# Linear attention then a gated feed-forward layer: the first three batches written in another order

## The chip, the core and the metric

The kernel runs on one core of a Trainium2 chip, as one program. The metric is device time in microseconds (us). The core has a matrix engine (TensorE, in rows PE, its weight loads PEld), VectorE (DVE), ScalarE (ACT), GpSimd (POOL, here mostly the issuer of loads) and SyncE (SP, here the issuer of stores and of transposing DMAs). Each engine runs its own instructions strictly in the order in which the program was written.

## The reference

```
phi(x) = elu(x) + 1
kv  = einsum(phi(k), v) per head;   z = sum of phi(k) over the tokens
att = (phi(q) @ kv) / (phi(q) . z + 1e-6)          # 8 batches, 8 heads, 576 tokens, 64 wide
x   = att as [4608 tokens, 512]
h   = x @ w_in                                     # 512 -> 2048
out = (h * sigmoid(beta * h)) @ w_out              # 2048 -> 512, float32
```

The inputs are float32. The kernel computes in bfloat16 with float32 sums: `h * sigmoid(beta*h)` is `silu(beta*h) / beta`, so each row of `w_out` is scaled by `1/beta` once and ScalarE's Silu does the rest.

## The kernel before, in words

**Tiling.** A batch's 576 tokens are 512 "main" tokens (four tiles of 128, t = 0 to 3) and a tail of 64 (t = 4). The eight tails are gathered in `xT_tail` and make a ninth piece of 512 tokens. For every piece there is an H phase (L282: 16 groups, ff = 0 to 15, of four 128x512 matmuls with `w_in`, each group evacuated by one Silu into `g`) and a Y phase (L307: four tiles t of 16 matmuls with `w_out`, each evacuated by one VectorE copy into `y_sb`, L319, and stored by SP, L299). Each phase is 64 matmuls. This text writes H0, Y0, H1 and so on, H8 and Y8 being the tails.

**Attention of one batch.** `elu` (L170): Exp of k and of q on ScalarE (L156), then on VectorE the max with 0 (L157), the min of the exponential with 1 (L159) and the sum (L160), for k and q each, and a copy of v beside a column of ones (L166). `attention` (L191): 20 matmuls that sum phi(k) times v (L204), masked by VectorE into `kv_bd` (L210); q transposed; for each t four "numerator" matmuls (L233) and on VectorE the denominator, its reciprocal and the product `xs` (L241, L242, L244); then `xs` transposed into `xT`, the input of H. Batches 0 and 1 transpose on TensorE (L222, L261, each evacuated by VectorE, L226, L265). From batch 2 on (`DMA_T = 2`, `by_dma`) q and `xs` are transposed by SP's DMAs (L185, L257).

**Order.** The program's order is written by hand: `h_phase` and `y_phase` call `step(fill)` after every group, and each call advances a generator of attention work by one `yield`. Batch 0's attention comes wholly before H0; batch 1's is spread from the second half of Y0 and finished by `drain` before H1; batch 2's from the start of Y1, with batch 3's `elu` beside it, both finished by `drain` before H2. For b >= 2 the attention of b+1 runs in H(b) and the `elu` of b+2 in Y(b).

**Loads and buffers.** All loads are issued by POOL, in order, with a conversion to bfloat16 (the blocks of `w_out` come as float32 into borrowed room: `g_sb[1]`, `xqk[2]` and `stage`, L106, and VectorE scales them into `w_out_sb`, L345). A POOL issue waits for the load that was issued eight before it. PSUM has four banks for H and Y (`mm`), one pair for numerators, and two for everything else. `xs` and `y_sb` have two buffers each.

## Time and profile before

| | us |
|---|---|
| median of 3 runs (lowest to highest) | 360.45 (356.15 to 363.02) |
| the profiled execution: its own time | 355.22 |
| its span in the profile | 353.4 |
| TensorE busy, of the span | 293.8 |
| VectorE, ScalarE, POOL busy | 143.7, 153.2, 48.0 |

The span runs from the first instruction to the last; the time has 1.8 us more. A busy TensorE may be running at either of its two clock levels, 1.2 or 2.4 GHz: a 128x512 matmul then takes about 0.43 or 0.22 us. The views used below are the page's parts, windows (busy time of each engine in stretches of the span), the timeline, groups of instructions by line, and waits by who waited for whom.

### The profile page before, as it was taken

To read this page: it belongs to the slowest core of one execution; us is meant where nothing else is said; L and a number is where in the kernel's file an instruction comes from. 1 tells how busy PE (TensorE), PEld (TensorE's weight loads), DVE (VectorE), ACT (ScalarE), POOL (GpSimd) and SP (SyncE) were. 2 spreads that over 40 slices of the span, in tenths; PEclk is the share of its full clock that TensorE was granted. 3 is DMA by queue.
4 is the path that set the end of the run, shared out by engine and by line. 5 is a ranking of instruction groups with operands and counts; after the bars stand their busy time and mean duration, and the time that the engine had idled before them with its cause. 6 is when DMAs were issued, how large, how long until landed. Compare 5 with 4: busy or idle time off the path is not lost.

```text
span 353.4 us, 4069 instructions
## 1 busy us (share of the span) xinstructions
PE 293.8 (83%) x1553; PEld 142.9 (40%) x1553; DVE 143.7 (41%) x281; ACT 153.2 (43%) x174; POOL 48.0 (14%) x64
## 2 busy tenths in 40 slices
...
GB/s 101 193 269 251 307 176 217 220 42 64 1 151 185 121 203 9 59 80 173 150 61 74 163 61 37 39 156 53 16 129 94 40 61 58 2 59 59 2 52 66
DMA packets 76467, 37.63 MB, mean 106 GB/s; under 512 B 44176, under 2 KB 70816, under 8 KB 76448
## 3 DMA queue, kind: packets, MB, share of 16 engines
...
q14 instruction: 7, 0.06, 0.1%
...
## 4 chain that ended last, share of the span: by engine, by line
PE 54%; DMA 9%; DVE 3%; ACT 1%; issue 1%; SPq 1%; DVEq 0%; ACTq 0%
PE h_ps L287 26%; PE y_ps L312 23%; DMA xT<-xs 4%; DMA xqk<-in_k_dram 3%; PE nps L233 2%; DMA out_dram<-y_sb 2%; PE kvp L204 2%; DVE y_sb L319 1%; SPq L185 1%; ACT e L156 1%; DVE xs L244 1%; DVE r L157 0%; DVE e L159 0%; DVE qk_p L160 0%; ACT L156 0%
## 5 line engine op out<-in xcount | busy, mean ns | idle before, releaser
L291 ACT ACTIVATE g<-h_ps,beta_c 128x512 bf16<-128x512 f32 x144 | 98.5, 687 | 107.3 <-PE h_ps L287 107.3
L287 PE MATMUL h_ps<-xT,w_in 128*128 128x512 bf16 x512 | 125.5, 396 | 7.5 <-DVE y_sb L319 4.5
L312 PE MATMUL y_ps<-w_out,g 128*128 128x512 bf16 x576 | 128.2, 382 | 0.0
L287 PEld LDWEIGHTS <-w_in 128*128 128x128 bf16 x576 | 56.1, 101 | 72.5 <-issue 16.7
L312 PEld LDWEIGHTS <-g 128*128 128x128 bf16 x576 | 56.5, 98 | 67.8 <-issue 1.7
L319 DVE COPY y_sb<-y_ps 128x512 f32<-128x512 f32 x36 | 24.5, 687 | 95.9 <-PE y_ps L312 71.6
L156 ACT ACTIVATE e<-xqk 128x2560 bf16<-128x2560 bf16 x16 | 36.7, 2331 | 4.4 <-DMA xqk<-in_q_dram 2.9
L291 ACT ACT_TABLE_LOAD x7 | 9.0, 1283 | 62.7 <-PE h_ps L287 62.7
L233 PE MATMUL nps<-kv_bd,q_pT 128*128 128x130 bf16 (+1 forms) x160 | 18.6, 247 | 18.9 <-DMA q_pT<-qk_p 10.8
L244 DVE TENSOR_TENSOR xs<-nps,rden 128x512 bf16<-128x512 f32 (+1 forms) x40 | 27.6, 690 | 7.1 <-DMA xT<-xs 5.9
L159 DVE TENSOR_SCALAR e<-e 128x2560 bf16<-128x2560 bf16 x16 | 13.3, 832 | 38.3 <-ACT e L156 38.3
L233 PEld LDWEIGHTS <-q_pT 128*128 128x128 bf16 (+1 forms) x160 | 13.2, 114 | 29.3 <-DVE xs L244 11.7
L160 DVE TENSOR_TENSOR qk_p<-r,e 128x2560 bf16<-128x2560 bf16 x16 | 23.9, 1493 | 0.5
L241 DVE TENSOR_SCALAR den<-nps 128x8 f32<-128x8 f32 (+1 forms) x40 | 6.6, 164 | 39.2 <-PE nps L233 38.8
L204 PE MATMUL kvp<-vaug,qk_p 128*128 128x130 bf16 x160 | 13.6, 243 | 8.4 <-DVE qk_p L160 8.4
L64 POOL DMA_DIRECT2D vraw<-in_v_dram x8 | 7.1, 888 | 82.7 <-DVE vaug L166 80.8
L204 PEld LDWEIGHTS <-qk_p 128*128 128x128 bf16 x160 | 12.1, 110 | 12.5 <-DVE qk_p L160 9.0
L287 PE MATMUL h_ps<-xT_tail,w_in 128*128 128x512 bf16 x64 | 14.0, 379 | 0.0
L261 PE MATMUL xtp<-identity,xs 128*128 128x128 bf16 (+1 forms) x40 | 5.4, 285 | 10.1 <-DVE xs L244 10.1
L157 DVE TENSOR_SCALAR r<-xqk 128x2560 bf16<-128x2560 bf16 x16 | 13.5, 842 | 0.0
L156 ACT ACT_TABLE_LOAD x7 | 9.0, 1283 | 8.0 <-DMA xqk<-in_k_dram 7.9
L64 POOL DMA_DIRECT2D xqk<-in_k_dram x8 | 7.5, 931 | 33.6 <-ACT e L156 20.7
...
## 6 DMA issues: line engine op xcount, KB each, us to landing
...
g<-in_moe_w_out_dram POOLq DMA_DIRECT2D x2, 1024.0 KB, 17.1
...
```

The lines of the kernel that those rows point to most:

```text
L64: nc.gpsimd.dma_start(out=dst[:, :, 0:NJ, :].rearrange("p h j d -> p h (j d)"), in_=src[b, :, 0:MAIN, :].rearrange("h (p j) d -> p h (j d) ...
L156: nc.scalar.activation(e, x, ACTF.Exp)
L157: nc.vector.tensor_scalar(r, x, 0.0, None, ALU.max)
L159: nc.vector.tensor_scalar(e, e, 1.0, None, ALU.min)
L160: nc.vector.tensor_add(st[b, "p"][:, a].rearrange("p j (h d) -> p h j d", h=H), r, e)
L204: nc.tensor.matmul(kvp[:, pp, :], qk_p[:, 1, j, p * P : (p + 1) * P], va[:, j, 2 * p : 2 * p + 2, 0 : D + 1], start=(j == 0), stop=(j == N ...
L233: nc.tensor.matmul(nps[:n, p // 2, o : o + 2 * (D + 1)], q_pT[:, t, p, :n], kv_bd[:, p, :], start=True, stop=True, skip_group_check=True,)
L244: nc.vector.tensor_mul(xs[t][:n], nv[:, :, :, 0:D], rden[:n, :, :, None].to_broadcast([n, 2, 4, D]),)
L287: nc.tensor.matmul(hp, w_in_sb[ff // 4][:, kc, (ff % 4) * P : (ff % 4 + 1) * P], x[:, :, kc, :] if b < B else x[:, kc, :], start=(kc == 0) ...
L291: nc.scalar.activation(g[:, ff, :], hp, ACTF.Silu, scale=beta_c[:, ff : ff + 1])
L312: nc.tensor.matmul(yp, g[:, ff, t * P : (t + 1) * P], w_out_sb[ff // 4][:, ff % 4, :], start=(ff == 0), stop=(ff == FC - 1),)
L319: nc.vector.tensor_copy(y_sb, yp)
```

## The change

Nothing that is computed changes. The generators and `step`, `drain`, `chain`, `wait`, `lazy` are replaced by small functions (one for each piece of a batch's attention) and by hand-written plans: dictionaries from a step of H or Y (the number of the group after which it runs) to the pieces to write there.

- Start: batch 0 is loaded as k, q, v; Exp, min and sum, and the copy of v run by halves of the heads; TensorE transposes q before and between the kv sums; the first three numerators come in a row in separate banks.
- H0 runs ff 0 to 7 for tokens t 0 and 1, then ff 0 to 7 for t 2 and 3, then ff 8 to 15 for all; the rest of batch 0's attention lies between its groups.
- `w_out` comes after batch 1's k, with batch 1's q and v between its blocks. Y0 (`y_phase_wide`) keeps four tiles open in four banks and goes by ff, so that a block of `w_out` is first needed when its ff comes up. The scaling of the four blocks is spread over H0 and Y0.
- Batch 1's attention lies in Y0, batch 2's in Y1, both with TensorE transposes (`DMA_T = 3`). From batch 3 on, q is transposed by DMA in H(b), and the numerators and the transposing DMAs of `xs` move from H(b) to Y(b).
- Transposed tiles on TensorE are evacuated by ScalarE (Copy), and so are two of Y0's four outputs.
- PSUM is four `mm` banks and four `att` banks; a tile's numerators take two `att` banks; `xs` has four buffers, `y_sb` three. VectorE's denominator and product are done by halves of the heads.

The diff, cut to its core:

```diff
-    DMA_T = 2
+    DMA_T = 3
...
-    numps = ctx.enter_context(tc.tile_pool(name="numps", bufs=1, space=bass.MemoryType.PSUM))
-    miscps = ctx.enter_context(tc.tile_pool(name="miscps", bufs=2, space=bass.MemoryType.PSUM))
+    attps = ctx.enter_context(tc.tile_pool(name="attps", bufs=4, space=bass.MemoryType.PSUM))
...
+    def mm_bank(shape, dtype=F32):
+        return mmps.tile(shape, dtype, tag="mm", name="mm")
+    def att_bank(shape, dtype=F32):
+        return attps.tile(shape, dtype, tag="att", name="att")
...
+    stage = consts.tile([P, 4 * DM], F32, name="stage")
...
+    w_out_f = [
+        a.rearrange("p (c m) -> p c m", c=4)
+        for a in (x_f[:, 0:2048], stage, g_f[:, 0:2048], g_f[:, 2048:4096])
+    ]
+    def load_w_out(i):
+        nc.gpsimd.dma_start(out=w_out_f[i], in_=w_out_v[:, i * 4 : (i + 1) * 4, :])
...
     load_k(0)
+    load_q(0)
     load_v(0)
-    load_q(0)
+    ident16 = consts.tile([FC, FC], F32)
+    make_identity(nc, ident16)
     identity = consts.tile([P, P], BF16)
     make_identity(nc, identity)
-    ident16 = consts.tile([FC, FC], F32)
-    make_identity(nc, ident16)
...
     for i in range(4):
         nc.gpsimd.dma_start(out=w_in_sb[i], in_=w_in_v[:, :, i * 512 : (i + 1) * 512])
...
-    w_out_f = [
-        a.rearrange("p (c m) -> p c m", c=4)
-        for a in (g_f[:, 0:2048], g_f[:, 2048:4096], x_f[:, 0:2048], stage)
-    ]
-    for i in range(4):
-        nc.gpsimd.dma_start(out=w_out_f[i], in_=w_out_v[:, i * 4 : (i + 1) * 4, :])
-        if i == 1:
-            load_q(1)
-            load_k(1)
+    load_k(1)
+    load_w_out(0)
+    load_w_out(1)
+    load_q(1)
+    load_w_out(2)
     load_v(1)
+    load_w_out(3)
...
+    def exp_(b, a, h0=0, h1=H):
+        if h0 == 0:
+            st[b, "e", a] = work.tile([P, H, NT, D], BF16, tag="e", name="e")
+        nc.scalar.activation(
+            st[b, "e", a][:, h0:h1], xqk[b % NX][:, a, h0:h1], ACTF.Exp
+        )
+    def relu(b, a):
+        st[b, "r", a] = work.tile([P, H, NT, D], BF16, tag="r", name="r")
+        nc.vector.tensor_scalar(st[b, "r", a], xqk[b % NX][:, a], 0.0, None, ALU.max)
...
+    def q_trans(b, t):
+        n = rows(t)
+        tp = att_bank([P, KC, P], BF16)
...
+        nc.scalar.activation(st[b, "qT"][:, t, :, :n], tp[:, :, :n], ACTF.Copy)
+    def q_trans_dma(b):
+        nc.sync.dma_start_transpose(
+            out=st[b, "qT"].rearrange("p t c n -> p (t c) n"),
+            in_=st[b, "p"][:, 0].rearrange("p j m -> p (j m)"),
+        )
...
+    def num_norm(b, t):
...
+        xs = work.tile([P, 2, 4, D], BF16, tag="xs", name="xs", bufs=4)
...
+        for i in range(2):
+            nc.vector.tensor_scalar(den[:n, i], nv[i][:, :, D], 1e-6, None, ALU.add)
+        nc.vector.reciprocal(rden[:n], den[:n])
+        for i in range(2):
...
+                xs[:n, i], nv[i][:, :, 0:D],
+                rden[:n, i, :, None].to_broadcast([n, 4, D]),
...
+        if by_dma(b):
+            nc.sync.dma_start_transpose(
+                out=x_dst(b, t), in_=xs.rearrange("p a h d -> p (a h d)")[:n]
+            )
...
+    def x_trans(b, t):
+        if by_dma(b):
+            return
...
+        nc.scalar.activation(x_dst(b, t), tp[:, :, :n], ACTF.Copy)
+    def run(plan, i):
+        for f in plan.get(i, ()):
+            f()
+    def h_phase(b, x, groups, plan):
         g = g_sb[b % 2]
...
+        for i, (ff, t0, t1) in enumerate(groups):
+            hp = mm_bank([P, 512])
+            c0, c1 = t0 * P, t1 * P
             for kc in range(KC):
                 nc.tensor.matmul(
...
+                    hp[:, c0:c1],
+                    w_in_sb[ff // 4][:, kc, (ff % 4) * P : (ff % 4 + 1) * P],
+                    x[:, t0:t1, kc, :] if b < B else x[:, kc, c0:c1],
                     start=(kc == 0), stop=(kc == KC - 1),
...
             nc.scalar.activation(
...
+                g[:, ff, c0:c1], hp[:, c0:c1], ACTF.Silu, scale=beta_c[:, ff : ff + 1]
...
+            run(plan, i)
...
+    def y_out(b, t, yp, on_act=False):
+        y_sb = work.tile([P, DM], F32, tag="y_sb", name="y_sb", bufs=3)
+        if on_act:
+            nc.scalar.activation(y_sb, yp, ACTF.Copy)
+        else:
+            nc.vector.tensor_copy(y_sb, yp)
+        store(b, t, y_sb)
+    def y_phase(b, plan):
...
+            yp = mm_bank([P, DM])
...
+                y_mm(b, yp, t, ff)
...
+                    run(plan, 4 * t + ff // 4)
+            y_out(b, t, yp)
+            run(plan, 4 * t + 3)
+    def y_phase_wide(b, plan):
+        yp = [mm_bank([P, DM]) for _ in range(4)]
+        for ff in range(FC):
+            for t in range(4):
+                y_mm(b, yp[t], t, ff)
+            run(plan, ff)
+        for t in range(4):
+            y_out(b, t, yp[t], on_act=(t % 2 == 1))
...
+    HH = H // 2
+    begin(0)
+    make_beta()
+    exp_(0, 1, 0, HH)
+    exp_(0, 1, HH, H)
+    relu(0, 1)
+    exp_(0, 0, 0, HH)
+    exp_(0, 0, HH, H)
+    phi(0, 1, 0, HH)
+    phi(0, 1, HH, H)
+    relu(0, 0)
+    phi(0, 0, 0, HH)
+    phi(0, 0, HH, H)
+    v_copy(0, 0, HH)
+    v_copy(0, HH, H)
+    q_trans(0, 0)
+    q_trans(0, 1)
+    kv_mm(0, 0, mm_bank)
+    q_trans(0, 2)
+    kv_mm(0, 1, mm_bank)
+    kv_mask(0, 0)
+    kv_mask(0, 1)
+    q_trans(0, 3)
+    q_trans(0, 4)
+    num_mm(0, 0)
+    num_norm(0, 0)
+    num_mm(0, 1)
+    num_norm(0, 1)
+    num_mm(0, 2, mm_bank)
+    num_norm(0, 2)
+    x_trans(0, 0)
+    x_trans(0, 1)
+    def F(f, *a):
+        return lambda: f(*a)
+    plan = {
+        1: [F(x_trans, 0, 2), F(num_mm, 0, 3), F(num_norm, 0, 3)],
+        3: [F(num_mm, 0, 4), F(num_norm, 0, 4)],
+        5: [F(x_trans, 0, 3)],
+        8: [F(x_trans, 0, 4)],
+        20: [F(w_out_scale, 0)],
+        22: [F(begin, 1), F(relu, 1, 1)],
+    }
+    h_phase(
+        0, xT[0],
+        [(ff, 0, 2) for ff in range(8)] + [(ff, 2, 4) for ff in range(8)]
+        + [(ff, 0, 4) for ff in range(8, FC)],
+        plan,
+    )
...
+    exp_(1, 1)
+    w_out_scale(1)
+    plan = {
+        1: [F(phi, 1, 1), F(exp_, 1, 0)],
+        5: [F(relu, 1, 0), F(w_out_scale, 2)],
+        7: [F(phi, 1, 0), F(v_copy, 1), F(load_next, 3)],
+        9: [F(q_trans, 1, 0), F(q_trans, 1, 1)],
+        10: [F(q_trans, 1, 2), F(kv_mm, 1, 0, att_bank), F(kv_mask, 1, 0)],
+        11: [F(kv_mm, 1, 1, att_bank), F(kv_mask, 1, 1), F(w_out_scale, 3),
+             F(q_trans, 1, 3), F(q_trans, 1, 4), F(num_mm, 1, 0), F(num_norm, 1, 0),
+             F(num_mm, 1, 1), F(num_norm, 1, 1)],
+        12: [F(x_trans, 1, 0), F(num_mm, 1, 2), F(num_norm, 1, 2)],
+        13: [F(x_trans, 1, 1), F(num_mm, 1, 3), F(num_norm, 1, 3)],
+        14: [F(x_trans, 1, 2), F(num_mm, 1, 4), F(num_norm, 1, 4)],
+        15: [F(x_trans, 1, 3)],
+    }
+    y_phase_wide(0, plan)
+    ALL = [(ff, 0, 4) for ff in range(FC)]
+    h_phase(1, xT[1], ALL, {
+        1: [F(x_trans, 1, 4)],
+        8: [F(begin, 2), F(relu, 2, 1)],
+        10: [F(relu, 2, 0)],
+        12: [F(v_copy, 2)],
+    })
...
+    exp_(2, 1)
+    exp_(2, 0)
+    y_phase(1, {
+        4: [F(phi, 2, 1)],
+        6: [F(phi, 2, 0)],
+        7: [F(kv_mm, 2, 0, att_bank)],
+        8: [F(kv_mask, 2, 0), F(kv_mm, 2, 1, att_bank)],
+        9: [F(kv_mask, 2, 1), F(q_trans, 2, 0), F(q_trans, 2, 1)],
+        10: [F(q_trans, 2, 2), F(q_trans, 2, 3)],
+        11: [F(q_trans, 2, 4), F(begin, 3), F(exp_, 3, 1), F(exp_, 3, 0), F(num_mm, 2, 0), F(num_norm, 2, 0)],
+        12: [F(num_mm, 2, 1), F(num_norm, 2, 1)],
+        13: [F(num_mm, 2, 2), F(num_norm, 2, 2), F(x_trans, 2, 0)],
+        14: [F(num_mm, 2, 3), F(num_norm, 2, 3), F(x_trans, 2, 1)],
+        15: [F(x_trans, 2, 2), F(x_trans, 2, 3)],
+    })
...
+        n = b + 1
+        plan = {}
+        if b == 2:
+            plan[0] = [F(num_mm, 2, 4), F(num_norm, 2, 4)]
+            plan[2] = [F(x_trans, 2, 4)]
+        if n < B:
+            plan[3] = [F(relu, n, 1), F(phi, n, 1)]
+            plan[5] = [F(relu, n, 0), F(phi, n, 0), F(q_trans_dma, n)]
+            plan[7] = [F(v_copy, n)]
+            plan[11] = [F(kv_mm, n, 0, att_bank)]
+            plan[12] = [F(kv_mask, n, 0), F(kv_mm, n, 1, att_bank)]
+            plan[13] = [F(kv_mask, n, 1)]
+        h_phase(b, xT[b % 3] if b < B else xT_tail, ALL, plan)
...
+        plan = {}
+        if n + 1 < B:
+            begin(n + 1)
+            exp_(n + 1, 1)
+            exp_(n + 1, 0)
+        if n < B:
+            for t in range(NT):
+                plan[1 + 2 * t] = [F(num_mm, n, t)]
+                plan[2 + 2 * t] = [F(num_norm, n, t)]
+        y_phase(b, plan)
```

**What moves on POOL, the issuer of loads,** from the last two blocks of `w_in` on. In the names, `xqk_73` and `vraw_76` before (`xqk_70` and `vraw_73` after) are batch 1's q, k and v. Before:

```order
L100 DMA w_in_81<-in_moe_w_in_dram 128x4x512
L100 DMA w_in_82<-in_moe_w_in_dram 128x4x512
L111 DMA g_92<-in_moe_w_out_dram 128x4x512 x2
L64 DMA xqk_73<-in_q_dram 128x8x256
L68 DMA xqk_73<-in_q_dram 64x8x64
L64 DMA xqk_73<-in_k_dram 128x8x256
L68 DMA xqk_73<-in_k_dram 64x8x64
L111 DMA xqk_74<-in_moe_w_out_dram 128x4x512
L111 DMA stage<-in_moe_w_out_dram 128x4x512
L64 DMA vraw_76<-in_v_dram 128x8x256
```

and after the change:

```order
L118 DMA w_in_78<-in_moe_w_in_dram 128x4x512
L118 DMA w_in_79<-in_moe_w_in_dram 128x4x512
L70 DMA xqk_70<-in_k_dram 128x8x256
L74 DMA xqk_70<-in_k_dram 64x8x64
L103 DMA xqk_71<-in_moe_w_out_dram 128x4x512
L103 DMA stage<-in_moe_w_out_dram 128x4x512
L70 DMA xqk_70<-in_q_dram 128x8x256
L74 DMA xqk_70<-in_q_dram 64x8x64
L103 DMA g_89<-in_moe_w_out_dram 128x4x512
L70 DMA vraw_73<-in_v_dram 128x8x256
L74 DMA vraw_73<-in_v_dram 64x8x64
L103 DMA g_89<-in_moe_w_out_dram 128x4x512
```

Batch 1's k is now ahead of `w_out`, and its q and v stand between the blocks.

**What moves on VectorE around Y0:** `L345` before and `L160` after are the scaling of `w_out`, `e`, `qk_p` and `r` are the elu of batch 1. Before:

```order
L345 TENSOR_SCALAR w_out_83<-g_92,rbeta 128x512 x4
L345 TENSOR_SCALAR w_out_84<-g_92,rbeta 128x512 x4
L345 TENSOR_SCALAR w_out_85<-xqk_74,rbeta 128x512 x4
L345 TENSOR_SCALAR w_out_86<-stage,rbeta 128x512 x4
L84 MEMSET xqk_74 64x16x32
L319 COPY y_sb<-y_ps 128x512
L157 TENSOR_SCALAR r<-xqk_73 128x2560
L319 COPY y_sb<-y_ps 128x512
L166 COPY vaug_78<-vraw_76 128x8x5x64
L159 TENSOR_SCALAR e<-e 128x2560
L160 TENSOR_TENSOR qk_p<-r,e 128x8x5x64
L157 TENSOR_SCALAR r<-xqk_73 128x2560
```

and after the change:

```order
L160 TENSOR_SCALAR w_out_80<-xqk_71,rbeta 128x512 x4
L185 TENSOR_SCALAR r<-xqk_70 128x2560
L90 MEMSET xqk_71 64x16x32
L160 TENSOR_SCALAR w_out_81<-stage,rbeta 128x512 x4
L189 TENSOR_SCALAR e<-e 128x2560
L190 TENSOR_TENSOR qk_p<-r,e 128x8x5x64
L185 TENSOR_SCALAR r<-xqk_70 128x2560
L160 TENSOR_SCALAR w_out_82<-g_89,rbeta 128x512 x4
L189 TENSOR_SCALAR e<-e 128x2560
L190 TENSOR_TENSOR qk_p<-r,e 128x8x5x64
L196 COPY vaug_75<-vraw_73 128x8x5x64
L216 TENSOR_TENSOR kv_bd<-att,kvmask 128x260 x2
L160 TENSOR_SCALAR w_out_83<-g_89,rbeta 128x512 x4
L264 TENSOR_SCALAR den<-att 128x4 x2
```

The third block's scaling (`w_out_82`) now stands behind batch 1's `qk_p` for k, which needs its Exp, and the fourth's behind the masks of the kv sums.

**What moves on SP around Y1 and H2:** before, from Y0's and Y1's first stores on:

```order
L299 DMA out_dram<-y_sb 128x512 x5
L185 DMA_TRANSPOSE q_pT<-qk_p 128x20x128
L299 DMA out_dram<-y_sb 128x512 x2
L257 DMA_TRANSPOSE xT_89<-xs 128x4x128 x2
L185 DMA_TRANSPOSE q_pT<-qk_p 128x20x128
L299 DMA out_dram<-y_sb 128x512
L257 DMA_TRANSPOSE xT_89<-xs 128x4x128 x2
L257 DMA_TRANSPOSE xT_tail<-xs 128x4x64
```

and after the change:

```order
L319 DMA out_dram<-y_sb 128x512 x8
L236 DMA_TRANSPOSE q_pT<-qk_p 128x20x128
L272 DMA_TRANSPOSE xT_84<-xs 128x4x128
L319 DMA out_dram<-y_sb 128x512
L272 DMA_TRANSPOSE xT_84<-xs 128x4x128 x2
L319 DMA out_dram<-y_sb 128x512
L272 DMA_TRANSPOSE xT_84<-xs 128x4x128
L272 DMA_TRANSPOSE xT_tail<-xs 128x4x64
```

All eight stores of Y0 and Y1 now come ahead of the first transposing DMA, which is batch 3's.

## Rows read from the trace of the kernel before

**Rows 1.** The page: its first line and part 1's TensorE row.
```profile
span 353.4 us, 4069 instructions
...
PE 293.8 (83%) x1553; PEld 142.9 (40%) x1553; DVE 143.7 (41%) x281; ACT 153.2 (43%) x174; POOL 48.0 (14%) x64
```

**Rows 2.** Windows by stage: busy us (instructions) per engine, TensorE clock, DMA share, GB/s.
```profile
0.00:32.00 32.00, 10.07 (x82) 7.85 (x82) 20.14 (x49) 7.24 (x4) 17.20 (x28) 1.00 1.18 204
32.00:47.70 15.70, 15.70 (x67) 6.76 (x66) 7.50 (x18) 10.31 (x15) 5.94 (x7) 1.00 1.35 251
47.70:61.40 13.70, 13.70 (x65) 6.21 (x64) 7.98 (x10) 7.82 (x5) 6.95 (x9) 1.00 1.50 206
61.40:75.20 13.80, 7.73 (x83) 5.70 (x80) 10.86 (x28) 0.00 (x0) 0.72 (x2) 0.68 1.23 171
75.20:91.50 16.30, 16.30 (x67) 6.94 (x66) 1.76 (x3) 10.31 (x15) 1.57 (x2) 0.85 0.32 37
91.50:132.70 41.20, 19.36 (x106) 9.10 (x105) 20.10 (x33) 11.21 (x6) 8.93 (x10) 0.78 1.04 142
132.70:263.30 130.60, 125.60 (x673) 60.74 (x674) 60.37 (x111) 72.09 (x80) 6.67 (x8) 0.97 0.45 82
263.30:293.40 30.10, 30.10 (x169) 14.78 (x168) 8.72 (x21) 12.18 (x17) 0.00 (x0) 1.00 0.28 79
293.40:349.40 56.00, 55.28 (x257) 24.85 (x254) 6.22 (x9) 22.00 (x32) 0.00 (x0) 1.00 0.13 38
```

**Rows 3.** Timeline, first 43 us: start, length, instruction, [idle before, and releaser].
```profile
7.94 1.28 ACT L156 ACT_TABLE_LOAD   x1 [7.94 <-DMA xqk<-in_k_dram]
...
11.34 1.13 DVE L166 COPY vaug<-vraw 128x2560 bf16<-128x2560 bf16 x1 [2.23 <-DMA vraw<-in_v_dram]
...
14.44 2.34 ACT L156 ACTIVATE e<-xqk 128x2560 bf16<-128x2560 bf16 x1 [2.87 <-DMA xqk<-in_q_dram]
...
27.49 0.89 POOL L64 DMA_DIRECT2D vraw<-in_v_dram  x1 [1.91 <-DMA g<-in_moe_w_out_dram]
...
30.18 0.69 POOL L68 DMA_DIRECT2D vraw<-in_v_dram  x1 [1.80 <-DMA g<-in_moe_w_out_dram]
...
39.79 1.67 DVE L345 TENSOR_SCALAR w_out<-xqk,rbeta 128x512 bf16<-128x512 f32 x4 [4.23 <-DMA xqk<-in_moe_w_out_dram]
...
42.25 1.89 DVE L345 TENSOR_SCALAR w_out<-stage,rbeta 128x512 bf16<-128x512 f32 x4 [0.79 <-DMA stage<-in_moe_w_out_dram]
```

**Rows 4.** The page, part 5: costliest groups, with mean ns of one.
```profile
L291 ACT ACTIVATE g<-h_ps,beta_c 128x512 bf16<-128x512 f32 x144 | 98.5, 687 | 107.3 <-PE h_ps L287 107.3
...
L156 ACT ACTIVATE e<-xqk 128x2560 bf16<-128x2560 bf16 x16 | 36.7, 2331 | 4.4 <-DMA xqk<-in_q_dram 2.9
...
L159 DVE TENSOR_SCALAR e<-e 128x2560 bf16<-128x2560 bf16 x16 | 13.3, 832 | 38.3 <-ACT e L156 38.3
...
L160 DVE TENSOR_TENSOR qk_p<-r,e 128x2560 bf16<-128x2560 bf16 x16 | 23.9, 1493 | 0.5
...
L241 DVE TENSOR_SCALAR den<-nps 128x8 f32<-128x8 f32 (+1 forms) x40 | 6.6, 164 | 39.2 <-PE nps L233 38.8
```

**Rows 5.** Groups by line with shapes kept apart, the same columns.
```profile
L244 DVE TENSOR_TENSOR xs<-nps,rden 128x512 bf16<-128x512 f32 x32 | 22.1, 692 | 5.6 <-DMA xT<-xs 4.6
...
L265 DVE COPY xT<-xtp 128x512 bf16<-128x512 bf16 x8 | 3.4, 425 | 3.7 <-PE xtp L261 3.7
...
L345 DVE TENSOR_SCALAR w_out<-g,rbeta 128x512 bf16<-128x512 f32 x8 | 3.2, 479 | 0.0
```

**Rows 6.** Waits, all engines: us in total, times, longest.
```profile
PE nps L233 <- DMA q_pT<-qk_p: 10.8, 1, 10.8
...
DVE y_sb L319 <- DMA out_dram<-y_sb: 19.7, 4, 6.7
...
PE h_ps L287 <- DVE y_sb L319: 4.5, 2, 3.0
```

**Rows 7.** The tile q_pT: time from issue to landing of its transposes.
```profile
DMA to landing us min/median/max: 4.9/6.1/11.9
```

258 lines of the change are left out of this document (82 added, 176 removed).

## The prediction

> **What bounds the kernel now.** First the page's head: TensorE is busy 293.8 of 353.4 us [rows 1]. The last four phases, with no attention beside them, take 55.28 us for 257 matmuls, 13.8 a phase, 0.86 a group of four [rows 2]; eighteen such phases are 249 us. So the bound is TensorE at full clock, and some 100 us lie beside it. Next the windows by stage, to see where [rows 2]: 32.0 us pass before H0, in which TensorE is busy for 10; H0 and the main part of Y0 run without a gap; 13.8 us of batch 1's attention stand alone (7.7 busy, granted clock 0.68); then comes H1; then Y1 with batch 2's attention takes 41.2 where its matmuls need 13.8. From H2 on there is little left: 130.6 us for eight phases with four batches of attention, and a clean pair H6, Y6 with one batch's attention inside is 30.1. Last the waits: in Y1 a numerator stood 10.8 us for q's transposing DMA, output copies stood 19.7 us in four waits for their store to free a buffer, and H phases stood 4.5 us behind such copies [rows 6]. The reader should see three lumps: the start, the attention between Y0 and H1, and Y1.
>
> **Start, up to H0.** q0 takes v0's place in the load queue, so k0 is there at 7.9, q0 at 11.3, v0 at 14.4 [rows 3]. ScalarE: table load 1.28, then four half Exps of 2.33/2 [rows 3, 4]: 9.2, 10.4, 11.6, 12.7, 13.9. VectorE: a half of min and sum is (0.83 + 1.49)/2 = 1.16 [rows 4]; k's halves end at 11.6 and 12.8, the max of q (0.83, taken as the min's) at 13.6, q's halves at 14.8 and 16.0, v's copy (1.13 [rows 3]) at 17.1. TensorE then does 20 transposes and 20 sums at the lower clock, 0.12 each (H6's pair has 40 such matmuls in 30.1 - 27.6 = 2.5 us, 0.06 each, at the upper one [rows 2]): 16.1 + 4.8 = 20.9, the first numerators 21.4. A tile's norm is now two denominators, a reciprocal and two half products: 0.16 x 2 + 0.2 + 0.69 [rows 4, 5] and 0.2 for starting two more instructions, 1.45. Two norms end at 24.3, the second transpose and its copy at 25.6. H0 starts at **25.6**, not 32.0.
>
> **ScalarE's copies.** No row shows a Copy on ScalarE. The nearest are VectorE's copy of the same tile, 0.43 [rows 5], and ScalarE's own Silu of the same width, 0.69 [rows 4]; I take 0.69, the same engine. On the path lie one before H0, one before H1 and four before H2, so the lower end would take 6 x 0.26 = 1.6 us off. The Trainium skill, "ScalarE: Activation LUTs", Rules for kernel authors, says to leave such plain operations to VectorE, as faster per element; by its figure for immediate scale (186 ns + 0.833 ns per element, section What ACT_TABLE_LOAD costs) a copy is an estimated 0.61 us, and the sum would be 0.5 us lower. That VectorE is faster speaks against this part, yet VectorE is what Y0 will wait for, and 0.43 x 12 copies there would cost more than they do on ScalarE.
>
> **H0.** 13.8, plus the 1.9 that the low clock cost H0 before (15.7 - 13.8 [rows 2]), plus twelve transposes and eight numerators between the groups at 0.12: 18.1, to 43.7. The half-width groups stream the same columns. In sum H0 ends 4 us earlier, not 6.4, as 2.4 of attention went inside.
>
> **Y0 and batch 1's attention.** Weight blocks land every 2.7 us and a q, k or v every 3.5 [rows 3]. From the end of w_in (24.8) the new order lands k1 28.3, w_out blocks 31.0 and 33.7, q1 37.1, block 2 39.8, v1 43.3, block 3 46.0: no load is late. But block 2 is scaled behind batch 1's phi(k) in VectorE's queue, and that Exp is behind all of H0's Silus. ScalarE: last Silu 44.6, table 45.9, Exps 48.2 and 50.5. VectorE: phi(k) 50.6, max 51.4, block 2 (4 x 0.48 [rows 5]) 53.3, phi(q) 55.6, v 56.5. TensorE: eight ff's end at 50.9; ff 8 waits for its slice, 51.9; after ff 9 (53.7) q's transposes wait for phi(q), 55.7; transposes, sums, ff 10 and 11 take it to 59.4. VectorE: masks 60.2, block 3 62.0, norms of two tiles 64.9, then three rounds of numerators, norm and handing over (0.25 + 1.45 + 0.2), 70.6, and the first output copy 0.69. H1 could begin at 71.9; in that stretch TensorE is idle by turns, as it was at 61.4 to 75.2, where the clock was at its lower level for part [rows 2]. Hidden in part by VectorE's chain, I add 1.6 (bounds 0 and 5): **73.5**, against 75.2.
>
> **H1 and Y1.** H1: 13.8, 0.2 for a transpose, and 1.7 for a slow start (bounds 0 and the 2.5 of before, 16.3 - 13.8 [rows 2]): 89.2. Y1 needs no DMA any more, so the 10.8 us wait goes. Eight groups and half the sums: 96.7; three groups, the other sums, 16 transposes: 100.9; one group, four transposes, the first numerators: 102.2. Now VectorE has an output copy (0.69) and four norms (5.8): 108.7. ScalarE meanwhile has batch 3's two Exps (102.8 to 107.5) ahead of four transposed tiles' copies, 2.8, so the last is there at 110.4. H2 starts at **110.6**, against 132.7: this stage gives 20 of the total.
>
> **H2 to the end.** Five pairs at 30.1 [rows 2] and 0.6 for batch 2's last tile: 151.1, against 160.7 from 132.7 to 293.4. The 9.6 are the waits for output buffers [rows 6], which go as q's long transposing DMA leaves the store's place on SP and `y_sb` has a third buffer, and H2's slow start. In Y each norm (1.45) has two groups (1.7) to hide behind. Then four phases, 56.0, and the tail, 4.0, as before.
>
> **Sum.** 25.6 + 18.1 + 29.8 + 15.7 + 21.4 + 151.1 + 56.0 + 4.0 = 321.7 of span, 1.8 around it: 323.5, against the profiled execution's 355.22. The median shown, 360.45, is 5 higher than that; part of that spread may come from the DMA waits that go, so I say **324**, and the range has room for the shift.
>
> **Rivals.**
> A, *q's transposes land late*. From batch 3 on q's DMA is issued some 7.1 us into H (a copy, then 2 x (0.83 + 2.32)) and needed 13.8 + 1.2 + 1.7 = 16.7 in: 9.6 us of slack. At the same place VectorE's copy of v frees the loads of three batches (v, k, q) on POOL. For it: landing took 4.9 to 11.9, the most beside loads [rows 7]; against it: the median is 6.1, and only three of the five have loads beside them. 3 x 2.3 = 7: **331**. The Trainium skill, "Trainium Kernel Development and Optimization", Key Constraints, says that DMAs from SP's and POOL's queues share the same 16 engines and interleave; by it A is to be expected, and the spread from 4.9 to 11.9 agrees.
> B, *the clock stays low* in Y0's second half and Y1's. For it: 0.68 and 0.78 in the two stages of interleaved attention [rows 2]. Against it: Y1's first half is dense, and the 0.78 held an 11 us wait that goes. Eight ff's at twice 0.86 are 6.9 more in Y0, as many in Y1, half behind VectorE: **331**.
> C, *Y0 runs as its blocks land*, as if VectorE's order did not hold them: H1 at 62.5, **312**. Against it: the order shows block 2 behind phi(k).
> D, *slower*: the late transposes of A as long as the one in Y1 before, 10.8 of waiting [rows 6], for each of five batches: 54 us, **377**. It outweighs the gain from a mean wait of 7.4 us a batch, thus from a landing of 17 us. Against it: no landing was over 11.9 [rows 7].
>
> **Numbers.** Forecast 0.64, A 0.15, B 0.11, C 0.05, D 0.05, of which 0.03 come out slower and 0.02 within 2%, about what a measurement here can tell from no change. The forecast's own bounds: the low clock's costs at nothing (-3.3), copies at 0.43 (-1.6) and no slow start at H0 (-1.9) give 317; nothing gained from H2 on (+9.6) 333, the median's shift another 3. Range 313 to 336, which takes in A and B. Faster 0.95, same 0.02, slower 0.03.
>
> **What would show it.** H0 from about 25.6; in Y0 a TensorE wait after ff 9 for phi(q); H1 near 73, H2 near 110 with ScalarE's copies behind batch 3's Exps; pairs of 30.1 from there. Wrong if numerators wait for `q_pT` in each Y (A), if Y0's matmuls take 0.43 us (B), or if H2 begins after 120.

## The result, and the profile after

The changed kernel takes **319.16 us** (median of 4 runs, 319.0 to 322.8) against 358.55 (median of 4, 356.15 to 363.02) in the same comparison: a ratio of 0.8946, 95% interval 0.8838 to 0.9053. Ratios leave out runs that are over 1.5% above the fastest of their kernel (here the one of 363.02), medians do not. The forecast was 324, range 313 to 336. The profiled execution's span is 317.0 us against 353.4 [rows 1]. First the head of the page after and part 1's TensorE row:

```profile
span 317.0 us, 4289 instructions
...
PE 286.5 (90%) x1625; PEld 144.0 (45%) x1625; DVE 142.9 (45%) x344; ACT 168.5 (53%) x216; POOL 46.7 (15%) x64
```

TensorE has 72 matmuls more (40 transposes of batch 2, 32 halves in H0) and is busy 7.3 us less, as it was granted the upper clock for more of its time (mean granted clock 0.987 for 0.942); the rest of the 36.4 us was idle time. Next the windows of the kernel after by stage, with the columns of [rows 2]; the stages are the start, H0, Y0 in two parts, H1, Y1, the pair H2 and Y2, four pairs, and the last phases:

```profile
0.00:24.60 24.60, 7.45 (x62) 5.87 (x63) 15.47 (x45) 9.85 (x13) 14.45 (x25) 1.00 1.19 163
24.60:41.60 17.00, 17.00 (x116) 11.27 (x116) 7.31 (x21) 14.18 (x27) 6.60 (x8) 0.90 1.31 294
41.60:53.60 12.00, 9.16 (x42) 3.82 (x41) 7.33 (x10) 6.59 (x5) 4.62 (x5) 1.00 1.48 227
53.60:68.50 14.90, 12.47 (x101) 7.52 (x102) 10.10 (x34) 5.03 (x10) 4.97 (x6) 0.89 1.58 190
68.50:84.05 15.55, 14.42 (x68) 6.30 (x69) 2.69 (x4) 12.15 (x19) 1.56 (x2) 1.00 0.58 109
84.05:103.90 19.85, 18.78 (x138) 10.18 (x137) 12.39 (x30) 15.61 (x16) 3.48 (x4) 1.00 0.63 101
103.90:136.40 32.50, 31.25 (x177) 15.05 (x177) 16.69 (x42) 18.16 (x21) 4.70 (x6) 1.00 0.80 125
136.40:257.10 120.70, 120.70 (x674) 59.16 (x672) 64.69 (x152) 64.93 (x77) 6.27 (x8) 1.00 0.50 97
257.10:312.40 55.30, 55.24 (x256) 24.85 (x254) 5.55 (x9) 22.00 (x32) 0.00 (x0) 1.00 0.13 39
```

Against [rows 2]: the start is 7.4 us shorter (24.6 for 32.0). From H0 to Y1's first matmul nothing is gained: 59.45 for 59.5. Y1 is 21.35 shorter (19.85 for 41.2), the five pairs from H2 on 7.5 (153.2 for 160.7), the end as long as before. 7.4 + 0 + 21.4 + 7.5 = 36.3 of the 36.4.

Now the two places that the forecast named. Y0 in the timeline of the kernel after (start, length, instruction, idle time before it and what ended that):

```profile
42.53 1.28 ACT L179 ACT_TABLE_LOAD   x1
43.83 4.57 ACT L179 ACTIVATE e<-xqk 128x2560 bf16<-128x2560 bf16 x2
46.20 0.83 DVE L189 TENSOR_SCALAR e<-e 128x2560 bf16<-128x2560 bf16 x1 [10.34 <-ACT e L179]
...
49.20 2.06 DVE L160 TENSOR_SCALAR w_out<-g,rbeta 128x512 bf16<-128x512 f32 x4
...
50.05 1.89 PE L328 MATMUL mm<-w_out,g 128*128 128x512 bf16 x8 [1.06 <-DVE w_out L160]
...
53.59 0.62 PE L228 MATMUL att<-identity,qk_p 128*128 128x128 bf16 x8 [1.65 <-DVE qk_p L190]
```

ScalarE is through with H0's Silus at 42.5, so VectorE stands 10.34 us for the Exp of k before it can do phi(k), and block 2 of w_out is scaled behind that. TensorE waits 1.06 for its slice, goes on to ff 9, and waits 1.65 for phi(q): the wait that the prediction put there, after ff 9. And the place before H2:

```profile
97.24 4.55 ACT L179 ACTIVATE e<-xqk 128x2560 bf16<-128x2560 bf16 x2
101.69 2.14 ACT L292 ACTIVATE xT<-att 128x512 bf16<-128x512 bf16 x4
...
103.89 1.02 PE L305 MATMUL mm<-xT,w_in 128*128 128x512 bf16 x4 [0.95 <-ACT xT L292]
```

Four transposed tiles' copies follow two Exps of batch 3 without a gap, and H2's first matmul waits for the last of them, as forecast. One wait was not forecast, in H1. Y0's four outputs come at once and `y_sb` has three buffers:

```profile
68.31 0.59 ACT L336 ACTIVATE y_sb<-mm 128x512 f32<-128x512 f32 x1
71.05 0.60 ACT L336 ACTIVATE y_sb<-mm 128x512 f32<-128x512 f32 x1 [2.14 <-DMA out_dram<-y_sb]
71.66 1.28 ACT L311 ACT_TABLE_LOAD   x1
...
71.69 1.02 PE L305 MATMUL mm<-xT,w_in 128*128 128x512 bf16 x4 [0.15 <-ACT y_sb L336]
73.69 1.67 PE L305 MATMUL mm<-xT,w_in 128*128 128x512 bf16 x7 [0.98 <-ACT g L311]
```

ScalarE's second output copy stands 2.14 us for a store, ahead of H1's table load and Silus in the same queue; TensorE then finds no free bank and waits 0.15 and 0.98 us.

Last the waits in the kernel after (us in total, times, longest), which answer to [rows 6]:

```profile
PE att L228 <- DVE qk_p L190: 11.0, 3, 8.4
...
ACT y_sb L336 <- DMA out_dram<-y_sb: 2.1, 1, 2.1
...
PE att L248 <- DMA q_pT<-qk_p: 1.2, 1, 1.2
```

And of the kernel after, as in [rows 7], the view of the tile `q_pT`, time from issue to landing:

```profile
DMA to landing us min/median/max: 4.9/8.7/10.2
```

The wait of 10.8 us, for batch 2's q, is gone with its DMA; the one that is left is 1.2, for batch 3's, in Y2. The first row is the wait for phi(q), 8.4 of its 11.0 us at the start and 1.65 in Y0. The output copies' 19.7 us and TensorE's 4.5 us behind them are gone but for the place in H1. The landing itself is no faster: the median went from 6.1 us (six transposes) to 8.7 (five).

### The profile page after: what moved, and what is told of

It reads as the page before. It is cut to its first block, busy times and chain, and to the rows that moved or that the text cites. A ratio compares the mean times of both kernels' runs of the same rounds, so it can differ in the third digit from the quotient of the medians.

```text
span 317.0 us, 4289 instructions
## 1 busy us (share of the span) xinstructions
PE 286.5 (90%) x1625; PEld 144.0 (45%) x1625; DVE 142.9 (45%) x344; ACT 168.5 (53%) x216; POOL 46.7 (15%) x64
## 4 chain that ended last, share of the span: by engine, by line
PE 80%; DVE 6%; DMA 6%; ACT 5%; issue 2%; POOL 0%; ACTq 0%; DVEq 0%; POOLq 0%
PE mm L305 37%; PE mm L328 35%; DMA q_pT<-qk_p 3%; PE att L248 3%; ACT e L179 3%; PE att L208 2%; DMA xqk<-in_k_dram 2%; DVE qk_p L190 1%; PE att L228 1%; DVE w_out L160 1%; DVE e L189 1%; ACT xT L292 1%; PE att L288 1%; ACT L179 1%; DMA out_dram<-y_sb 1%
## 5 line engine op out<-in xcount | busy, mean ns | idle before, releaser
L328 PE MATMUL mm<-w_out,g 128*128 128x512 bf16 x576 | 133.5, 381 | 1.2 <-DVE w_out L160 1.1
L311 ACT ACTIVATE g<-mm,beta_c 128x512 bf16<-128x512 f32 (+1 forms) x152 | 98.0, 666 | 54.2 <-PE mm L305 53.9
L305 PE MATMUL mm<-xT,w_in 128*128 128x512 bf16 (+1 forms) x544 | 116.2, 369 | 3.4 <-ACT xT L292 2.3
L338 DVE COPY y_sb<-mm 128x512 f32<-128x512 f32 x34 | 23.4, 690 | 91.1 <-PE mm L328 91.0
L179 ACT ACTIVATE e<-xqk 128x2560 bf16<-128x2560 bf16 (+1 forms) x18 | 36.7, 2091 | 0.1
L267 DVE TENSOR_TENSOR xs<-att,rden 128x256 bf16<-128x256 f32 (+1 forms) x78 | 29.4, 418 | 1.3
L190 DVE TENSOR_TENSOR qk_p<-r,e 128x2560 bf16<-128x2560 bf16 (+1 forms) x18 | 24.2, 1345 | 0.6
L189 DVE TENSOR_SCALAR e<-e 128x2560 bf16<-128x2560 bf16 (+1 forms) x18 | 13.5, 751 | 11.9 <-ACT e L179 11.9
L248 PE MATMUL att<-kv_bd,q_pT 128*128 128x130 bf16 (+1 forms) x156 | 17.0, 234 | 1.9 <-DMA q_pT<-qk_p 1.2
L305 PE MATMUL mm<-xT_tail,w_in 128*128 128x512 bf16 x64 | 14.0, 379 | 0.0
## 6 DMA issues: line engine op xcount, KB each, us to landing
xqk<-in_q_dram POOLq DMA_DIRECT2D x8, 512.0 KB, 11.6
```

The costliest lines, as they stand in the source:

```text
L179: nc.scalar.activation(st[b, "e", a][:, h0:h1], xqk[b % NX][:, a, h0:h1], ACTF.Exp)
L189: nc.vector.tensor_scalar(e, e, 1.0, None, ALU.min)
L190: nc.vector.tensor_add(st[b, "p"][:, a].rearrange("p j (h d) -> p h j d", h=H)[:, h0:h1], st[b, "r", a][:, h0:h1], e,)
L248: nc.tensor.matmul(nps[:n, pp * 2 * (D + 1) : (pp + 1) * 2 * (D + 1)], st[b, "qT"][:, t, p, :n], st[b, "kv"][:, p, :], start=True, stop=Tr ...
L267: nc.vector.tensor_mul(xs[:n, i], nv[i][:, :, 0:D], rden[:n, i, :, None].to_broadcast([n, 4, D]),)
L305: nc.tensor.matmul(hp[:, c0:c1], w_in_sb[ff // 4][:, kc, (ff % 4) * P : (ff % 4 + 1) * P], x[:, t0:t1, kc, :] if b < B else x[:, kc, c0:c1 ...
```

## Experiments: from the kernel before

Experiments 1, 2, 4 and 5 ran on one chip, 6 to 9 on a second, 3 and 10 to 12 on a third, each time beside the kernel before. The changed kernel did not run beside them, so against it stand the ratios and the spans of the profiled executions.

**1. One number, DMA_T.** Batch 2's q and x transposed on TensorE, all else as before.

```diff
-    DMA_T = 2
+    DMA_T = 3
```

> The kernel before with one number changed: batch 2 is transposed on TensorE too, with the old generators, two-bank pool and two buffers. Theory W (waits): most of Y1's 41.2 us was time spent waiting for transposing DMAs, 10.8 us for q and about 8 for xs and xT, so the stage from Y1 to H2 falls to 24 to 30 us and the whole is 11 to 17 us faster (ratio 0.955 to 0.97). Rival O (order): the gain of the whole change comes from the hand-written plans; the old drain still leaves batch 2's attention alone after Y1, as batch 1's 13.8 us were, so the stage stays above 35 us and the whole is within 2% of before.

339.67 us (337.53 to 341.17), ratio 0.9447 [0.9365, 0.9529] to the kernel before: theory W, and rival O falls. The window from Y1 to H2:

```profile
91.20:120.90 29.70, 20.27 (x143) 10.86 (x145) 23.19 (x42) 11.28 (x7) 8.60 (x10) 0.94 1.06 135
```

It takes 29.7 us in place of 41.2, though its 40 matmuls of transposes and their copies come on top. The span fell by 14.4 us (to 339.0), within the 11 to 17 expected; the ratio is lower than the 0.955 to 0.97.

**2. One number, the buffers of `y_sb`.**

```diff
-            y_sb = work.tile([P, DM], F32, tag="y_sb", name="y_sb")
+            y_sb = work.tile([P, DM], F32, tag="y_sb", name="y_sb", bufs=3)
```

> The kernel before with three output buffers instead of two. Theory W: the 19.7 us of output copies waiting for a store go, and with them the 4.5 us that H phases waited; five pairs from H2 on fall from 160.7 to 154 or less, the whole is 4 to 8 us faster. Rival S (the queue of SP): stores stand behind q's transposing DMA, which holds SP for 3 to 6 us, so a third buffer only moves the wait to the next copy; less than 2 us of gain.

352.77 us, ratio 0.9831 [0.9772, 0.989]. Windows of Y1 and of the five pairs, then TensorE's wait and the row of the tile `q_pT`:

```profile
91.90:136.50 44.60, 19.26 (x103) 9.10 (x103) 20.09 (x33) 11.25 (x7) 8.92 (x10) 0.75 1.03 131
136.50:290.60 154.10, 153.13 (x830) 74.96 (x841) 69.69 (x132) 84.22 (x97) 6.65 (x8) 0.98 0.44 85
...
PE nps L233 <- DMA q_pT<-qk_p: 14.1, 1, 14.1
...
DMA to landing us min/median/max: 4.9/6.1/15.2
```

The five pairs take 154.1 us for 160.7: W, and rival S falls. Y1, which had to stay as it was, became 3.4 us longer (44.6): the transposing DMA that it waits for landed after 15.2 us, where it took 11.9 before [rows 7], and TensorE stood 14.1 us for it, for 10.8. Why it landed later was not tried.

**3. Both numbers.**

> The kernel before with two of its numbers changed: DMA_T 3 (batch 2's transposes on TensorE) and three buffers of y_sb; nothing else of the change. Alone, the first took the span from 353.4 to 339.0 and the second the five pairs from H2 to Y6 from 160.7 to 154.3. Theory W (both take away waits of their own place): they add. Y1's start to H2 stays near 30, the five pairs fall from 158.0 to 152.5-154.5, span 333-336, time 333-337, so some 23-26 of the 39 us of the change come from two numbers. Rival D (what one takes away, the other's wait comes back in its place, since both are set by SP's queue): time 338-341, five pairs still 157-158.

336.44 us (336.16 to 337.96), ratio 0.9472 [0.9416, 0.9529]. Windows of this kernel: start, H0 to Y1, Y1 to H2, five pairs.

```profile
0.00:32.40 32.40, 10.08 (x82) 7.87 (x82) 20.18 (x49) 7.24 (x4) 17.80 (x28) 1.00 1.19 205
32.40:91.50 59.10, 53.06 (x273) 25.69 (x273) 28.20 (x58) 28.40 (x35) 14.79 (x18) 0.88 1.07 163
91.50:121.10 29.60, 20.18 (x142) 10.87 (x143) 23.19 (x42) 11.24 (x7) 8.59 (x10) 0.94 1.04 133
121.10:274.50 153.40, 152.30 (x833) 74.45 (x841) 69.99 (x133) 84.22 (x97) 6.70 (x8) 0.99 0.47 90
```

The pairs are down to 153.4, as in the changed kernel, and Y1 to H2 to 29.6: theory W, and rival D falls. By the spans of the profiled executions the two numbers are worth 18.8 us (353.4 to 334.6) of the whole change's 36.4, by the ratios 5.3% of 10.5%: half of it, less than the 23 to 26 of 39 us expected. What is left between this kernel and the changed one is 17.6 us of span: 7.8 before H0 and 9.8 in Y1 to H2. Experiments 6 and 7 take the first further apart. The second was not taken apart: the order of the work, ScalarE's copies and the PSUM banks all differ there, and which of them brings it is open.

## Experiments: from the changed kernel

**4. Two buffers of `y_sb`, as before** (`bufs=3` to `bufs=2`).

> The changed kernel with two output buffers instead of three. Theory S' (SP's order is what counts): with q's DMA moved into H nothing long stands before a store, so two buffers cost only at the end of Y0, where four outputs come at once: H1 is held 2 to 4 us longer, pairs from H3 on stay at 30.2. Theory W: the third buffer is what took the waits of the pairs away; pairs go back to 31 to 33, the whole is 7 to 10 us slower.

320.29 us, ratio 0.8923 [0.887, 0.8977], which can't be told from the changed kernel's. The pairs stay at 30.2 us from H3 on: theory S'. H1 takes 16.4 us for 15.6, held 0.8 longer and not the 2 to 4 expected. So here the third buffer isn't what frees the H phases: with SP's new order two suffice, as q's long DMA no longer stands between the copies and their stores (that it is this move, and not another of the order's, is argued and was not tried by itself). In experiment 2 the third buffer sufficed with the DMA in its old place. Each cures the same wait, and together they gain no more than one.

**5. Every evacuation on VectorE** (both `nc.scalar.activation(..., ACTF.Copy)` of transposed tiles become `nc.vector.tensor_copy`, and Y0's outputs too).

> The changed kernel with all evacuations of transposed tiles, and two outputs of Y0, back on VectorE. Theory V (VectorE bounds Y0): copies of 0.43 us come into the chain of norms; the stretch from q's transposes in Y0 to H1 (14.9 us) grows by 2 to 4, Y1's by 0 to 2, the whole is 2 to 5 us slower. Rival (plain copies belong on VectorE, where one takes 0.43 and not 0.60): the handing over gets shorter, Batch 3's Exps no longer stand ahead of the copies, and the whole is 0 to 3 us faster.

318.74 us, ratio 0.8888 [0.8829, 0.8948], 0.6% under the ratio of the changed kernel with intervals that overlap: no difference that can be told. Theory V, that it would cost 2 to 5 us, is not borne out; its trace does not rule out a smaller cost. In it H0 starts 0.5 us later (TensorE waits 1.53 in place of 0.69 for VectorE's copy of x) and H2 1.6 earlier; the pair H2 to Y2 then waits 2.6 us for `q_pT`, in place of 1.2, and takes 33.7 for 32.4 (from H2's first matmul to H3's). H0's 15.3 us, for 17.0, is no gain of the copies: it had the granted clock at 1.00 throughout, while the changed kernel's was 0.50 (1.2 GHz) from about 25.3 to 28.7, after waits of 0.55 and 0.69 us that experiment 11 had as well, without a drop; experiment 12, with the same copies as here, has 17.0 again. The clock was 1.00 in Y0 too, worth another 1.6 us (see 6). So of some 3.3 us that the clock gave, H2's start shows 1.6.

**6. H0 in full width**: the numerators of all five tiles of batch 0 and four of their five transposes ahead of sixteen groups of 512 columns, no halves.

```diff
...
-        [(ff, 0, 2) for ff in range(8)] + [(ff, 2, 4) for ff in range(8)]
-        + [(ff, 0, 4) for ff in range(8, FC)],
+        [(ff, 0, 4) for ff in range(FC)],
```

> The changed kernel with H0 in full width: all four token tiles are transposed before its first group. Theory H (halves pay little): H0 starts 2 to 4 us later but has 1.5 to 2.5 us less of attention inside, so Y0 starts 0.5 to 2 us later and the whole is 0 to 2 us slower. Rival: the halves bring the whole 7.4 us by which H0 starts earlier; the whole is 4 us or more slower.

318.71 us (median of three runs, 317.92 to 319.57; a fourth took 777.22, and no trace tells why), ratio 0.8919 [0.8874, 0.8964]: theory H, and the rival falls. H0 starts 2.2 us later, Y0 0.7, and H1 comes 1.2 us *earlier*. The windows from the end of phi(q) to H1, first of the changed kernel, then of this one:

```profile
53.53:68.47 14.94, 12.45 (x101) 7.51 (x101) 10.14 (x34) 5.00 (x10) 4.97 (x6) 0.89 1.58 190
...
53.91:67.23 13.32, 10.85 (x100) 6.71 (x101) 10.08 (x34) 4.99 (x10) 4.97 (x6) 1.00 1.58 192
```

The same instructions take 14.9 us at a mean granted clock of 0.89 (it was 0.50 from 62.8 to 66.3) and 13.3 at 1.00. With these 1.6 us taken out H1 would come 0.4 later here, so the halves bring H0 forward and hardly anything behind it. Whether they caused that clock was not tried; 4 and 7, which have them, show 0.89 and 0.88 in this place, 5, 9 and 10, which have them too, 1.00.

**7. The old order of loads** (k, v, q; blocks 0 and 1 of w_out, then q1 and k1, blocks 2 and 3, v1).

> The changed kernel with the load order of before: k, v, q for batch 0, and batch 1 behind the first two blocks of w_out, v last. Theory L (only the first three loads count): q of batch 0 lands 3.1 us later, H0 starts 1.5 to 3 us later; around Y0 no load was late, so the stretches from H0 to H2 stay within 0.7 us; the whole is 1 to 3 us slower. Rival: batch 1's place among the w_out blocks is needed for Y0's attention; Y0 to H1 grows by 3 us or more.

320.91 us, ratio 0.8978 [0.8945, 0.9011]. H0 2.2 us later and all behind it shifted by 1.6 to 2.4 (span 319.4 for 317.0): theory L, by the trace; the ratio alone does not tell it from the changed kernel. Experiments 6 and 7 took back 2.2 us each of the start's 7.4; the other 3 were not taken apart.

**8. Y0 tile by tile**, with all of w_out scaled ahead of batch 1's elu (`y_phase` in place of `y_phase_wide`, `w_out_scale(2)` and `(3)` before the plan).

> The changed kernel with Y0 one tile after the other, as in other batches, and all scaling of w_out ahead of batch 1's elu on VectorE. Theory E (what ends Y0 is phi(q), then the chain of norms, not the landing of w_out): TensorE waits about 2 us for block 3 in the first tile, phi(q) is ready at the same time as now (53 to 54), and two of VectorE's scalings are out of the chain of norms; H1 starts within 1.5 us of 68.5, the whole within 1%. Rival (the wide Y0 earns its four banks): Y0 stands until block 3 is scaled, and H1 starts 4 us or more later.

316.02 us, ratio 0.8837 [0.879, 0.8885]: theory E, and better. H1 came 2.6 us earlier and H2 4.0, of which the next pair gave 2.4 back (34.8 us). Phi(q) was ready 0.75 later (54.3); from there to H1 it took 11.6 us for 14.9. Of these 3.3 us 1.6 goes with the granted clock, 1.00 here (see 6), and most of the rest with block 3's scaling, 2.07 us that no longer stand ahead of the norms. H1 itself took 14.1 for 15.6, as Y0's outputs no longer come at once. The timeline of the next pair:

```profile
108.61 3.26 SPq L236 DMA_TRANSPOSE q_pT<-qk_p  x1
...
119.51 0.41 PE L248 MATMUL att<-kv_bd,q_pT 128*128 128x130 bf16 x4 [1.98 <-DMA q_pT<-qk_p]
119.75 3.09 PE L328 MATMUL mm<-w_out,g 128*128 128x512 bf16 x8
```

q's DMA is issued once phi(q) is done, and TensorE waits 1.98 us for it, then runs the next eight matmuls in 3.09 us, which take 1.89 at the upper clock.

**9. Block 2 scaled ahead of phi(k)**, Y0 still over four banks.

```diff
+    w_out_scale(2)
...
-        5: [F(relu, 1, 0), F(w_out_scale, 2)],
+        5: [F(relu, 1, 0)],
```

> The changed kernel with block 2 of w_out scaled ahead of batch 1's phi(k) on VectorE, where VectorE is idle for 10.3 us. Theory Q (VectorE's queue is what holds Y0): the wait of 1.1 us for w_out goes, phi(q) is ready 2 us earlier, H1 starts 1.5 to 2.5 us earlier and the whole is as much faster. Rival (ScalarE holds it: Exp of q ends at 48.4, and the chain of norms sets the end): H1 starts less than 0.7 us earlier.

319.5 us, ratio 0.8938 [0.8888, 0.8988]: theory Q's first half, and not its second. H1 started at 65.1 for 68.5, more than the 1.5 to 2.5 us expected: phi(q) was ready 1.35 earlier (52.2), and 1.6 of the rest goes with the clock, 1.00 in Y0 here (see 6). And H1 lost it: 19.6 us for 15.6.

```profile
70.42 0.60 ACT L336 ACTIVATE y_sb<-mm 128x512 f32<-128x512 f32 x1 [4.88 <-DMA out_dram<-y_sb]
...
71.07 1.02 PE L305 MATMUL mm<-xT,w_in 128*128 128x512 bf16 x4 [2.88 <-ACT y_sb L336]
```

The four outputs come 3.4 us earlier, but the store whose buffer the last one needs landed 5.3 us after issue, where it took 2.5: 4.88 us of standing where it was 2.14.

**10. The same with four buffers of `y_sb`.**

> The changed kernel with w_out's block 2 scaled ahead of phi(k) of batch 1, as before, and four buffers of y_sb in place of three. With three, H1 was reached 3.4 us earlier, but took 19.7 us in place of 15.6, with ScalarE's output copy 4.88 us behind a store. Theory B (the buffer was the wait): each of Y0's four outputs has its own, H1 is back to 15.6-16.0, Y1 starts at 80.5-81.5, H2 at 100-101.5; the span falls to 313.5-315.5, as the next place (q_pT's landing in Y2) gives back some 2. Rival H (the stores would hold ScalarE or TensorE in another way): H1 stays at 18-20, span 317-318.

313.64 us (312.93 to 314.15), ratio 0.8819 [0.877, 0.8868]. Theory B, and better: the span is 312.4 for the 313.5 to 315.5 expected. The rows of the same place:

```profile
64.66 1.08 ACT L336 ACTIVATE y_sb<-mm 128x512 f32<-128x512 f32 x2
65.76 1.28 ACT L311 ACT_TABLE_LOAD   x1
```

Both copies follow each other without a wait; H1 takes 14.1 us (15.6 to 16.0 expected), Y1 starts at 79.0, and the pair H2 to Y2 takes 32.9, with 1.8 us for `q_pT`.

**11. Experiment 8, and q ahead of k from H2 on.**

```diff
-            plan[3] = [F(relu, n, 1), F(phi, n, 1)]
-            plan[5] = [F(relu, n, 0), F(phi, n, 0), F(q_trans_dma, n)]
+            plan[3] = [F(relu, n, 0), F(phi, n, 0), F(q_trans_dma, n)]
+            plan[5] = [F(relu, n, 1), F(phi, n, 1)]
```

> The changed kernel with Y0 tile by tile and w_out scaled first, as in the run before, and from H2 on q's elu and its transposing DMA ahead of k's. There the DMA of q_pT was issued at 108.6, when phi(q) was done, and TensorE waited 1.98 us for it at 117.5, then ran 3 us at the lower clock; the pair H2 to Y2 took 34.8 us, where 30.2 is the pair without waits. Theory G (gains of the early stages are given back at q_pT's landing): issued 2.5-3 us earlier, it lands before it is wanted; the pair takes 30.2-32.0, the span is 311.5-313.5, time 312-314. Rival C (the DMA engines are busy with the loads of batch 5 there, and it lands when those are through): the wait stays over 1 us, the pair 33.5-35, time 315.5-317; phi(k) being later could also make TensorE wait at H's step 11 for it (rival K: a new wait of 0.5-1 us in each of five H phases, time 316-320).

313.4 us (312.78 to 314.71), ratio 0.8816 [0.8764, 0.8868]. Theory G: the pair takes 30.9 us for 34.8, without a wait for `q_pT` or, in any H, for phi(k) (so no K). The DMA's issue at 107.02 stands 5.7 us into H2, where it stood 8.7 in experiment 8. The pair's window, and a row from the tile's view:

```profile
101.30:132.20 30.90, 30.79 (x174) 15.03 (x176) 16.69 (x42) 18.16 (x21) 4.70 (x6) 1.00 0.85 132
...
DMA to landing us min/median/max: 4.9/5.7/6.5
```

Issued 3.9 us ahead of the loads that v's copy frees, it lands in 4.9 to 5.9 us for the three batches that have such loads, where it took 8.8 to 10.8 in experiment 8. In this trace Y0 began 2.2 us earlier than in 8 (H0 at 1.00) and waited it out, 3.71 us for block 3, which is scaled when it has landed, at 45.64 in both. Behind that wait the granted clock was 0.50 from 46.9 to 50.3, and phi(q) and H1 came 1.4 us later than in 8: what this run gains on 8 it gains in the pair. A narrow Y0 can't begin its first tile's end before that; the wide one can.

**12. Experiment 11 with VectorE's evacuations and four buffers.**

> As the run before (Y0 tile by tile, w_out scaled first, q's elu and DMA ahead of k's), with every evacuation of a transposed tile on VectorE and four buffers of y_sb. VectorE's evacuations alone had brought H0's length down by 1.7, Y0's by 1.0 and H2's start by 1.6, and all was given back in the pair H2 to Y2. Theory G (it was given back at q_pT's landing, and nowhere else): with that wait gone these are kept, H2 at 97-99, span 308.5-311.5, time 309-312. Rival V (VectorE is the longer queue in Y0 once w_out's 16 scalings stand ahead): TensorE waits more for phi(q) and for xs in Y0 and Y1, H2 at 99.5-101, time 312-315, no better than the run before it.

315.15 us (314.22 to 316.55), ratio 0.8874 [0.8813, 0.8935], 1.75 us over 11 in the same comparison: theory G falls, and rival V fits, by the time and by H2, which starts at 100.8, for 101.3, not at 97 to 99. The row of TensorE's waits that grew:

```profile
PE mm L305 <- DVE xT L292: 4.1, 3, 1.5
```

With the copies on VectorE, x's last tiles stand behind four norms and an output copy, and H0, H1 and H2 each wait for them (2.3 us in 11, for ScalarE's). The two profiled executions are 314.22 and 314.71, so the traces show how it comes about and not the 1.75.

The two fastest, 10 and 11, beat both kernels: spans of 312.4 and 312.9 us for the changed kernel's 317.0, though the intervals of their ratios still touch its own. Their gains lie in different places (Y0, where 1.6 is the clock's, and H1; Y2), and q ahead of k on top of 10 was not run; from 32.9 and 30.9 for the pair, an estimate is 2 us less than 313.6.

## Why the prediction was right, and where its sizes were off

**Start.** H0 at 24.57 for 25.6. The norm of a tile was taken as 1.45 (its terms make 1.41, and no row shows the 0.2 for starting two more instructions); the second one shows 0.22 + 0.20 + 0.76 = 1.18, and 1.26 from start to end. Transposes ran earlier than the sum had them (q's from 15.2, for 16.1). The order of the loads was worth 2.2 of the 7.4 (7).

**ScalarE's copies.** A Copy of 128x512 from PSUM took 0.60 us, the nearest row taken was Silu's 0.69, and VectorE's is 0.43. The Trainium skill, "ScalarE: Activation LUTs", What ACT_TABLE_LOAD costs, gave an estimate of 0.61: the trace agrees. The Trainium skill's rule on the same page, Rules for kernel authors, to use VectorE for relu, max, min, add and mul, which the prediction took to hold for a copy too, was not borne out here: experiment 5 was no faster that could be told, and 12 was slower. That the engine with the shorter queue at that place decides, and not the price, fits 12's waits and was not shown apart.

**H0, Y0 and batch 1.** H0 17.06 for 18.1. The 1.9 in it for a low clock was there: 17.06 is 1.7 above the 15.35 of experiment 5. [rows 2] has a clock of 1.00 in H0 of the kernel before, but its matmuls show the slow start that the prediction took from its length (ns of one: shortest, median, longest):

```profile
L287 PE MATMUL h_ps<-xT,w_in x9: 577/634/634, 32.0 to 35.4; 128*128 128x512 bf16 x9
...
L287 PE MATMUL h_ps<-xT,w_in x18: 379/379/379, 36.2 to 39.9; 128*128 128x512 bf16 x18
```

The first nine start 0.43 us apart, the next 18 0.22, which are the two clock levels; so a 1.00 in that column alone does not show the upper one.

Y0 to H1 took 26.84 for 29.8. The order of waits was right to the instruction, and phi(q) was ready 11.9 us after Y0's start, as forecast; it came at 53.5 and not 55.6 because Y0 began earlier. What was too long lay behind it, 14.9 us for 17.9. The three rounds of numerators and norm were taken as 5.7 with 1.6 for a low clock on top; they took 5.7 with a low clock in them, and 4.1 without it in experiment 6. So the 1.6 was of the right size, and the rounds were not. Two norms took 2.4 for 2.9, and 0.6 lies between the 71.9 written and the 71.3 that 70.6 and 0.69 make. Y0 did stand behind VectorE, thus rival C (312) fell; experiment 10, with block 2 ahead of phi(k) and a buffer for each output, comes near its time, and 1.6 of that goes with the clock.

**H1 and Y1.** 15.58 for 15.7, a right number for a wrong reason, thus by luck: no slow clock (1.00), but the store that ScalarE waited for. The prediction gave VectorE's copies three buffers and did not ask what four outputs at once do. Y1 to H2 19.84 for 21.4, with the forecast's wait and cause; the 10.8 us wait went, as 1 showed apart.

**H2 to the end.** 153.2 for 151.1. Four pairs at 30.17 as forecast; the first at 32.4, where `q_pT` landed 10.2 us after issue and TensorE waited 1.25: rival A in one batch of five. The landing was late in the three batches that have loads beside it (10.2, 9.2 and 8.7 us, for 4.9 in the other two), but the slack of 9.6 that the rival's sum gave covered two of them. In H2 the slack was 9.0: the DMA was issued 8.6 us into the phase and not 7.1, as batch 2's last norm stood ahead, and was needed after 17.6. The cause named, loads that v's copy frees at the same place, is what 11 shows: issued ahead of them the DMA lands in 4.9 to 5.9. The Trainium skill, "Trainium Kernel Development and Optimization", Key Constraints, states that the DMAs of SP's and POOL's queues interleave on the same 16 engines: 8.7 to 10.2 us beside loads and 4.9 without them agree. Rival D needed a mean landing of 17 and fell; rival B fell too, as one low stretch in Y0 cost 1.6 us and not 6.9, and Y1 had the clock at 1.00.

**The sum.** Six of the eight terms came out below what was written, the five pairs 2.1 above and the tail 0.6: 317.0 for 321.7. The median's shift of 5 between the profiled execution of before and its median did shrink: after, three of four runs lie within 0.3 of the profiled one's 319.0. That it went with the DMA waits is not shown: experiment 2's four runs lie within 0.8 us with Y1's wait still there, experiment 1's within 3.6 with it gone.
